# The last 128 dims of the first x chunk: a DMA transposition replaced by a row load and four matmuls

## The chip, the cores and the metric

The kernel runs on one core of a Trainium2 chip. The metric is the device time of one execution in microseconds. The profile is one execution on the chip; its times count from the start of the profiled span. TensorE (PE) multiplies, ScalarE (ACT), VectorE (DVE) and GpSimd (POOL) work on tiles, and SyncE (SP) issues nearly all DMAs; ScalarE issues a few at the start on a queue of its own.

## What is computed

One input x of 2048 tokens by 448 dims goes two ways, and a gate mixes the results:

```
x = A_x
g = sigmoid((x * gate_w).sum(-1, keepdims=True))
a = A_ref(x, wq, wk, wv, wo, beta)   # 16 heads of 28 dims, 4 segments of 512 tokens
b = B_ref(x, w1, b1, w2, b2)         # layernorm, then an MLP over the token axis, F = 1792
return g * a + (1 - g) * b
```

In A each segment has causal softmax attention inside it (`p = softmax(q k^T * scale + mask)`, `a_dot = p v`), and a linear memory of the segments before it (`a_mem = phi(q) M / phi(q) z`). Both are mixed by a sigmoid of beta per head and go through wo. B normalizes x over its dims, multiplies over tokens with w1 (`u = h^T w1 + b1`), applies gelu and multiplies with w2. All inputs are bf16.

## The kernel before

**Two forms of x.** The projections q, k and v contract over dims, so they need x with dims on the partitions: `xT`, four chunks `c` of up to 128 dims by 2048 tokens. The chunks begin at dims 0, 128, 256 and 320 (`C0`, line 21), so the last two overlap. The layernorm and the MLP need x with tokens on the partitions: `xh`, 16 tiles of 128 tokens. `xT` is made by DMA transpositions straight from memory (`transpose_x`, line 533). For each block `tc` of 512 tokens there are two: `dtx{tc}_0` for chunks 0 to 2, and `dtx{tc}_1` for chunk 3. Each is a resource of its own, `R_xT[tc][0]` and `R_xT[tc][1]`. `xh` is loaded by `load_x` (line 519), four tiles at a time: `ldx0`, `ldx4`, `ldx8`, `ldx12`.

**The order of the work.** Every operation has a name and is put in a list with what it reads and writes (`Sched.op`). A table `ORDER` (lines 304 to 376) gives the order of the names on each engine, written out in full. `@4` behind a name is the PSUM bank that it takes out of banks 4 to 7; `u0-7*6` is six matmuls from number 7 on. `Sched.plan` follows the table, and `finalize` puts semaphore waits where an operation reads what another engine or a DMA made. Each engine works through its row in order. On TensorE, `mm` (line 279) issues all matmuls of projections and MLP, so they all bear line 282.

**The start, on TensorE.** `warm` is nine 512-wide matmuls on constants into bank 3 (line 651). `gtr` (lines 839 and 840) transposes the gate's weights, which `gw` on VectorE copies out. `warm2` is one more warm-up. Then the v projection of token tiles 0 to 3: `pra0` to `pra3` take chunk 0 and the first piece of wv, `prb0` to `prb3` chunk 1 and the second piece. `lot2`, `lot0`, `prt0` to `prt3` take chunks 2 and 3 with the rest of wv. A group is made by `pair` (line 680). Of chunks 2 and 3, which overlap, each pair of tiles uses one as a whole and 64 rows of the other; the two halves run side by side in the array (`lo`, 64 rows, which the profile shows as 64\*128). After v come the k and q projections of block 0 (`prk0_*`, `prx0_3`, `prq0_*`), which wait for weights that VectorE copies into a padded form (`padk`, `padx`, `padq`, line 662), and then block 1. Scores of the first segment (`sc0_*`, line 973), block 2's k projections (`prk2_*`) and the MLP (`u*`) are interleaved behind them. `prk2_1`, the first of block 2, waits for both transpositions of that block. ScalarE turns scores into exponentials (`exp0_*`, line 982), out of PSUM banks 0 to 3, which the next scores use again. The scores are shown as 28\*128.

**The start, on the DMA queues.** SyncE's row begins `dtx0_0 dtx0_1 ldwk0 ldwk1 ldwq0 ldwqb dtx1_0 dtx1_1 ldx0 ldx4 ldx8 ldbeta ldw1_0_0 dtx2_0 ldx12 dtx2_1`. ScalarE issues the four pieces of wv, a piece of wk, and small loads (lines 525, 529, 546, 555, 557).

Of the kernel before, what the change touches and what calls it, by code (L numbers as in the profile page):

```python
# [12 lines left out]
D = 448  # L13
# [292 lines left out]
warm gtr@4 warm2 pra0@7 pra1@4 pra2@5 pra3@6 prb3 prb2 prb0 prb1 lot2 lot0 prt1 prt3 prt2 prt0 pra0_1 pra0_2 pra0_0  # L306
btr@7 lok0_0 lok0_2 prk0_0 prx0_3 prk0_2 prk0_1 prt7@4 prx1_3@5 prk1_2@6 lot6@7 lok1_2 loq0_0 loq0_2 prq0_2 prq0_0
prt6 prq1_2@4 prq0_2h prq1_1@5 prq1_2h@6 loq1_0@7 loq1_2 prq0_1 prq1_0 prk1_1@4 sc0_0 lok1_0@5 lot4@67 prk1_0 prt5
prt4 sc0_1 prk2_1@4 prx2_3@5 prk2_2@6 lok2_2 lok2_0@7 sc0_2 prk2_0 u1-0@6*5 u0-0@4 u1-5 u0-1*2 u2-0@5*3 sc0_3 u0-3
u2-3*2 u0-4*2 u3-0@7*2 u0-6 u2-5*2 u3-2 u1-6 sc0_4 u1-7 u0-7*6 u3-3 u0-13 u2-7 u3-4 u0-14*2 u1-8 sc1_0 u1-9*6 u2-8*2  # L310
u1-15 u2-10*4 u3-5*2 u4-0@4 u3-7*2 sc1_1 u5-0@6*2 u2-14 u5-2*2 u2-15 u3-9*6 u5-4 u3-15 u4-1*5 u5-5*2 pv1@5 u4-6*2
sc1_2 u4-8 u5-7*5 u4-9*4 u5-12 pv0@7 u5-13 sc1_3 u4-13*3 u6-0@5*3 u7-0@7 u6-3 u5-14 u6-4*2 u5-15 u6-6 sc1_4 u6-7
u7-1 u6-8*4 u7-2*2 u6-12 u7-4*3 u6-13*3 sc2_0 u7-7*7 pv2@4 u7-14*2 sc2_1 mst0@6 u8-0@4*2 prq2_1@5 prq2_0@7 loq2_0
sc2_2 u8-2*4 prq2_2@5 u8-6*4 prq2_2h@6 loq2_2 mem1 u8-10*2 u9-0@5 u8-12 u9-1*8 u8-13*2 u11-0@6 sc2_3 u9-9*3 pv3@7
u9-12 u8-15 u9-13*2 u11-1 u9-15 u11-2*4 sc2_4 u10-0@7*3 u11-6*6 u13-0@4 u10-3 pv4@5 sc3_0 u10-4*12 u11-12 u13-1
sc3_1 u13-2*3 u11-13*2 u13-5*2 pv5@5 u11-15 prt9@7 u13-7*4 sc3_2 lot8@5 u13-11*2 u12-0@6*5 prt8 u13-13*3 u12-5 sc3_3
lot10@57 u12-6*3 prt11 u12-9*7 prt10 sc3_4 mst1@7 prk3_1@4 pv6@6 prk3_0@7 lok3_0 sc4_0 prq3_1@5 prq3_0@7 wo0@6
# [7 lines left out]
y10-10*2 y11-9*3 y10-12 y11-12*2 lw14@45 y10-13 wo14 wo15 wo12@7 y12-0@6*2 lw12@5 wo13 y13-0@4*4 y15-0@7 y13-4*2  # L325
y14-0@5*2 y13-6*4 y12-2 y14-2*2 y13-10 y14-4 y12-3*2 y13-11 y12-5*3 y14-5 y15-1 y12-8*3 y14-6*3 y13-12*2 y12-11*3
y14-9*5 y15-2*12 y15-0#1@4 y15-1#1 y15-2#1 y15-3#1 y15-4#1 y15-5#1 y15-6#1 y15-7#1 y15-8#1 y15-9#1 y15-10#1 y15-11#1
# [25 lines left out]
ag7 fin5 mq3_3 phq3_2 oa10 ta11 rec11 msta2 phq3_3 oa11 mstc2 om11 tm12 tm13 tm14 tm15 ot11 ot10 cpv15 cpv14 eps13
fin4 ta12 eps15 gcol3 b2g2 eps12 omg3 rec12 oa12 fin6 ag8 om12 ta13 ot12 rec13 fin7 om13 oa13 o13 ot13 eps14 fin8
ag10 ta14 rec14 om14 oa14 ta15 rec15 om15 oa15 b2g3 fin9 ot14 ot15 fin11 fin10 fin13 fin12 fin14 fin15 fin15#1""",
# [9 lines left out]
dtx0_0 dtx0_1 ldwk0@0 ldwk1 ldwq0@1 ldwqb dtx1_0 dtx1_1 ldx0 ldx4 ldx8 ldbeta ldw1_0_0 dtx2_0 ldx12 dtx2_1 ldw1_0_1  # L365
# [13 lines left out]
def build_kernel(nc, X, WQ, WK, WV, WO, BETA, W1, B1, W2, B2, GW, OUT):  # L379
# [139 lines left out]
    def load_x(eng, t0, n):  # L519
        op(eng, lambda e: e.dma_start(xh[:, t0 : t0 + n, :], xv[:, t0 : t0 + n, :]),  # L520
           writes=R_x[t0 : t0 + n], name=f"ldx{t0}", dma=True, cost=500, nbytes=n * 128 * 896, prio=-3)
# [310 lines left out]
    def do_gw():  # L832
# [5 lines left out]
        def fn(e):  # L838
# [456 lines left out]
```

## Time and profile before

| what | us |
|---|---|
| median of three runs | 170.68 |
| lowest and highest of the three | 170.39, 171.07 |
| the profiled execution | 170.68 |
| its span, from the first to the last instruction | 168.9 |
| TensorE busy in the span | 164.7 |
| VectorE busy | 136.7 |
| ScalarE busy | 130.6 |
| GpSimd busy | 64.3 |

A matmul's duration runs from its issue to its modelled end; the next one can start before that, so the distance between starts tells the rate. PEld are the weight loads, which run beside matmuls. An engine name with q behind it (SPq, ACTq) is the engine's issuing side: the duration is the time that the issue took, not the transfer. `t` stands for any tile of the kernel. "t<-t L282" and the like name the line and not the operation, so operations are told by their time, their shape and their place in the row.

### The profile page before, as it was taken

To read this page: it belongs to the slowest core of one execution; us is meant where nothing else is said; L and a number is where in the kernel's file an instruction comes from. 1 tells how busy PE (TensorE), PEld (TensorE's weight loads), DVE (VectorE), ACT (ScalarE), POOL (GpSimd) and SP (SyncE) were. 2 spreads that over 40 slices of the span, in tenths; PEclk is the share of its full clock that TensorE was granted. 3 is DMA by queue.
4 is the path that set the end of the run, shared out by engine and by line. 5 is a ranking of instruction groups with operands and counts; after the bars stand their busy time and mean duration, and the time that the engine had idled before them with its cause. 6 is when DMAs were issued, how large, how long until landed. Compare 5 with 4: busy or idle time off the path is not lost.

```text
span 168.9 us, 4944 instructions
## 1 busy us (share of the span) xinstructions
PE 164.7 (98%) x2022; PEld 78.5 (47%) x2026; DVE 136.7 (81%) x321; ACT 130.6 (77%) x164; POOL 64.3 (38%) x100
## 2 busy tenths in 40 slices
PE   8999999999999999999999999999999999999994
PEld 2334444444554644544453454444454444564553
DVE  0088999877989989999999999999999978695042
ACT  0359999999999997999999998988985788604100
POOL 5000245260442524142177356445837355540000
PEclk9999999999999999999999999999999999999999
DMA  6998999888699945994337302328853129831202
GB/s 144 249 258 289 248 153 246 160 228 226 138 167 254 222 101 146 163 213 124 109 98 169 82 4 65 94 82 111 244 148 110 46 70 280 229 103 60 84 27 82
DMA packets 53974, 25.44 MB, mean 151 GB/s; under 512 B 18416, under 2 KB 53712, under 8 KB 53952
## 3 DMA queue, kind: packets, MB, share of 16 engines
q1 hardware_dynamic: 53160, 24.54, 61.2%
q10 hardware_dynamic: 792, 0.58, 1.7%
q8 instruction: 16, 0.26, 0.7%
q14 instruction: 6, 0.05, 0.1%
HBM read 18.82 MB, written 2.36 MB: 125 GB/s over the span
## 4 chain that ended last, share of the span: by engine, by line
PE 94%; DMA 3%; ACTq 1%; issue 1%; POOL 0%; DVE 0%; POOLq 0%
PE t L282 79%; PE t L973 8%; PE t L1003 5%; DMA t<-in_A_wv_dram 3%; PE t L856 1%; PE t L1076 1%; ACTq L525 1%; ACTq L546 0%; DVE t L1165 0%; POOL t L544 0%; POOL t L620 0%; POOL t L587 0%; POOL t L619 0%; POOL t L615 0%; POOLq L1280 0%
## 5 line engine op out<-in xcount | busy, mean ns | idle before, releaser
L282 PE MATMUL t<-t 128*32 128x448 bf16 (+9 forms) x1257 | 140.4, 352 | 1.0 <-issue 0.6
L282 PEld LDWEIGHTS t<-t 128*32 128x32 bf16 (+2 forms) x1261 | 63.7, 97 | 63.8 <-issue 15.3
L982 ACT ACTIVATE t<-t 128x2048 bf16<-128x2048 f32 x40 | 75.2, 1879 | 6.8 <-PE t L973 6.2
L985 POOL TENSOR_SCALAR_AFFINE_SELECT t<-t 128x512 bf16<-128x512 bf16 x64 | 43.3, 688 | 43.0 <-ACT t L982 40.0
L1040 POOL TENSOR_TENSOR t<-t 128x448 bf16<-128x448 f32 (+2 forms) x13 | 13.3, 1026 | 19.0 <-DVE t L1033 14.4
L1165 DVE SCALAR_TENSOR_TENSOR t<-t 128x448 bf16<-128x448 f32 (+2 forms) x17 | 10.7, 642 | 10.6 <-PE t L282 10.5
L973 PE MATMUL t<-t 28*128 28x512 bf16 (+3 forms) x256 | 15.8, 301 | 0.0
L1017 DVE STREAM_TRANSPOSE t<-t 128x512 f32<-128x512 f32 x16 | 11.3, 706 | 2.9 <-PE t L1003 2.7
L925 POOL TENSOR_TENSOR t<-t 128x4 f32<-128x4 f32 x4 | 4.2, 1054 | 23.4 <-DVE t L923 21.4
L1119 ACT ACTIVATE t<-t 128x448 bf16<-128x448 f32 x10 | 7.1, 732 | 7.6 <-PE t L282 7.6
L1003 PE MATMUL t<-t 128*32 128x512 bf16 (+3 forms) x256 | 11.5, 300 | 0.0
L1059 DVE STREAM_TRANSPOSE t<-t 128x512 bf16<-128x512 bf16 x16 | 10.9, 690 | 0.0
L973 PEld LDWEIGHTS t<-t 28*128 28x128 bf16 x256 | 4.4, 92 | 14.0 <-ACT t L982 7.7
L818 ACT ACTIVATE t<-t 128x448 bf16<-128x448 f32 x13 | 6.8, 546 | 4.2 <-PE t L282 4.2
L916 DVE BATCH_NORM_STATS2 t<-t 128x6 f32<-128x448 bf16 x16 | 9.3, 610 | 0.7 <-DMA t<-in_A_x_dram 0.7
L1145 DVE SCALAR_TENSOR_TENSOR t<-t 128x448 f32<-128x448 f32 x14 | 9.0, 649 | 0.7 <-ACT t L1140 0.6
L1003 PEld LDWEIGHTS t<-t 128*32 128x32 bf16 x256 | 6.7, 96 | 5.3 <-issue 0.7
L1137 ACT ACTIVATE t<-t 128x448 f32<-128x448 f32 x14 | 8.8, 638 | 0.1
L779 ACT ACTIVATE t<-t 128x512 bf16<-128x512 bf16 x12 | 7.6, 635 | 1.4 <-DVE t L736 1.4
L808 DVE SCALAR_TENSOR_TENSOR t<-t 128x512 bf16<-128x512 bf16 x12 | 8.5, 712 | 0.1
L1143 DVE TENSOR_SCALAR t<-t 128x448 f32<-128x448 f32 x10 | 6.5, 676 | 2.4 <-ACT t L1137 2.3
L1033 DVE SCALAR_TENSOR_TENSOR t<-t 128x448 f32<-128x448 f32 x12 | 8.4, 699 | 0.0
(76 smaller groups left out, 132.1 us busy)
## 6 DMA issues: line engine op xcount, KB each, us to landing
t<-in_B_w_dram SPq DMA_DIRECT2D x52, 256.0 KB, 3.9
t<-in_A_x_dram SPq DMA_DIRECT2D x4, 448.0 KB, 5.4
out_dram<-t SPq DMA_DIRECT2D x15, 112.0 KB, 2.0
t<-in_B_w_dram SPq DMA_DIRECT2D x8, 128.0 KB, 2.5
t<-in_A_wv_dram ACTq DMA_DIRECT2D x4, 112.0 KB, 4.1
t<-in_A_wq_dram SPq DMA_DIRECT2D x1, 336.0 KB, 4.8
spare_heads<-t SPq DMA_DIRECT2D x8, 32.0 KB
spare_heads<-t SPq DMA_DIRECT2D x16, 16.0 KB
```

Source lines behind the costliest of these rows:

```text
L282: last = e.matmul(out[q], w[:, q], x, skip_group_check=True, **kw)
L916: op("DVE", lambda e: e.bn_stats(st6[:, t, :], xh[:, t, :]), reads=[R_x[t]], writes=[R_st6[t]], name=f"bns{t}", cost=512, prio=P_PROJ - 10 ...
L973: last = e.matmul(bank(hl)[:, c0 : c0 + w], kT[r, hg, s * 512 + j * 128 : s * 512 + j * 128 + 128], qT[r, hg, s * 512 + 128 * j : s * 512 ...
L982: op("ACT", lambda e: e.activation(pslot(g), ps[:, 0:4, :], ACT.Exp, scale=SCALE), reads=R_bank[0:4], writes=[g.res], take=g, name=f"exp{p ...
L985: op("POOL", lambda e, c0=c0: e.affine_select(pslot(g)[:, :, c0 : c0 + 128], pslot(g)[:, :, c0 : c0 + 128], pattern=[[0, 4], [1, 128]], co ...
L1003: last = e.matmul(bank(cb)[32 * ((hl + hg) % 4) : 32 * ((hl + hg) % 4) + 32, 128 * j : 512], vaug[:, 4 * s + j, 32 * h : 32 * h + 32], psl ...
L1017: dv(lambda e: e.transpose(tt[:, ia, :], bank(cb)[:, 0:512]), [bres(cb)], [R_tt[ia]], "ta", 630, use=(cb,))
L1040: return e.tensor_tensor(dst, part(n3[0]), part(n3[1]), op=ALU.add)
L1059: dv(lambda e: e.transpose(oT[:, hg, s * 512 : s * 512 + 512], o), [R_ob[hg]] + ([R_obx] if hg else []), qres(hg, s), "ot", 635)
L1137: op("ACT", lambda e: e.activation(gg[:, q, :], bank(b)[:, 0:D], ACT.Square, bias=b1s[:, ft : ft + 1], scale=math.sqrt(GC)), **buse(b), re ...
L1145: op("DVE", lambda e: e.scalar_tensor_tensor(gg[:, q, :], gg[:, q, :], 1.0, vh[:, q, :], op0=ALU.add, op1=ALU.mult), reads=[R_gg[q], R_vh[ ...
L1165: op("DVE", lambda e: e.scalar_tensor_tensor(outst[:, p, c0:c1], bank(b)[:, 0 : c1 - c0], omg[:, T : T + 1], ag(T)[:, c0:c1], op0=ALU.mult ...
```

## The change

For block 0, chunk 3 of `xT` no longer comes from a DMA transposition. `dtx0_1` is dropped. In its place the last 128 dims (320 to 447) of the first four tiles of `xh` are loaded as rows by a DMA of its own, `ldxl`, which is the first on SyncE's queue. Later `ldx0` loads only the first 320 dims of those tiles. When `ldxl` has landed, TensorE multiplies each of the four 128 by 128 tiles with an identity matrix (`xtl`, into bank 2), and VectorE copies the four results into `xT` (`cpxl`). `warm2` has two matmuls instead of one. The layernorm's `bns0` to `bns3` read `ldxl`'s columns too.

```
+    R_xl = R("xl")
+
-    def load_x(eng, t0, n):
-        op(eng, lambda e: e.dma_start(xh[:, t0 : t0 + n, :], xv[:, t0 : t0 + n, :]),
-           writes=R_x[t0 : t0 + n], name=f"ldx{t0}", dma=True, cost=500, nbytes=n * 128 * 896, prio=-3)
+    def load_x(eng, t0, n, c0=0, c1=D, writes=None, name=None):
+        op(eng, lambda e: e.dma_start(xh[:, t0 : t0 + n, c0:c1], xv[:, t0 : t0 + n, c0:c1]),
+           writes=writes or R_x[t0 : t0 + n], name=name or f"ldx{t0}", dma=True, cost=500, nbytes=n * 256 * (c1 - c0), prio=-3)
...
-        for k, (c, n) in enumerate(((0, 3), (3, 1))):
+        for k, (c, n) in enumerate(((0, 3), (3, 1))[: 2 if tc else 1]):
...
+    load_x("SP", 0, 4, C0[3], D, [R_xl], "ldxl")
     transpose_x(0)
...
-    load_x("SP", 0, 4)
+    load_x("SP", 0, 4, 0, C0[3])
...
-    warm_up(1, "warm2", P_PROJ + 0.01, 3500.0)
+    warm_up(2, "warm2", P_PROJ + 0.01, 3500.0)
...
+    def last_dims():
+        def fn(e):
+            for t in range(4):
+                last = e.matmul(bank(2)[:, t * 128 : t * 128 + 128], xh[:, t, C0[3] : D], ident[:, :], start=True, stop=True,
+                                skip_group_check=True)
+            return last
+
+        op("PE", fn, reads=[R_xl, R_ident], writes=[R_bank[2]], name="xtl", mode="f", cost=4 * pe_cost(128), prio=P_PROJ - 1)
+        op("DVE", lambda e: e.tensor_copy(xT[:, 3, 0:512], bank(2)[:, 0:512]), reads=[R_bank[2]], writes=[R_xT[0][1]],
+           name="cpxl", cost=dve_cost(512), prio=P_BASE)
```

The table's rows are rewritten with few moves. One line of TensorE's and one of SyncE's, before and now:

```
-warm gtr@4 warm2 pra0@7 pra1@4 pra2@5 pra3@6 prb3 prb2 prb0 prb1 lot2 lot0 prt1 prt3 prt2 prt0 pra0_1 pra0_2 pra0_0
+warm gtr@4 warm2 xtl pra0@4 pra1@5 pra2@6 pra3@7 prb3 prb2 prb0 prb1 lot2 lot0 prt1 prt3 prt2 prt0 pra0_1 pra0_2
-dtx0_0 dtx0_1 ldwk0@0 ldwk1 ldwq0@1 ldwqb dtx1_0 dtx1_1 ldx0 ldx4 ldx8 ldbeta ldw1_0_0 dtx2_0 ldx12 dtx2_1 ldw1_0_1
+ldxl dtx0_0 ldwk0@0 ldwk1 ldwq0@1 ldwqb dtx1_0 dtx1_1 ldx0 ldx4 ldx8 ldbeta ldw1_0_0 dtx2_0 ldx12 dtx2_1 ldw1_0_1
```

Elsewhere the table moves single matmuls inside the MLP (`u2-8`, `u6-6` one place ahead of a group of scores or of another `u`; `y15-0` some ten places later) and a few neighbours on VectorE and SyncE.

TensorE's row at the start of the program, before (L651 is the warm-up, L839 and L840 the gate, the 449-wide matmuls the v projection of block 0, the 512-wide ones the k projection, L887 the biases):

```order
L651 MATMUL t<-const-bfloat16-1.0 128x512 x9
L839 MATMUL t<-t 128x3
L840 MATMUL t<-t 128x1
L651 MATMUL t<-const-bfloat16-1.0 128x512
L282 MATMUL t<-t 128x449 x16
L282 MATMUL t<-t 128x512 x6
L887 MATMUL t<-t 128x30
```

The same place now, in the changed file's line numbers (L655 is the warm-up, L843 and L844 the gate, L854 the new `xtl`):

```order
L655 MATMUL t<-const-bfloat16-1.0 128x512 x9
L843 MATMUL t<-t 128x3
L844 MATMUL t<-t 128x1
L655 MATMUL t<-const-bfloat16-1.0 128x512 x2
L854 MATMUL t<-t 128x128 x4
L282 MATMUL t<-t 128x449 x16
L282 MATMUL t<-t 128x512 x6
L902 MATMUL t<-t 128x30
```

One warm-up and four narrow matmuls stand between the gate and the first matmul of the v projection; what follows is in the order that it had.

SyncE's row from its start, before (L535 are the transpositions of x, L525 and L529 the weights wk and wq, L520 the loads of `xh`):

```order
L535 DMA_TRANSPOSE t<-in_A_x_dram 128x3x512
L535 DMA_TRANSPOSE t<-in_A_x_dram 128x1x512
L525 DMA t<-in_A_wk_dram 128x2x448
L525 DMA t<-in_A_wk_dram 128x448
L525 DMA t<-in_A_wq_dram 128x3x448
L529 DMA t<-in_A_wq_dram 128x448
L535 DMA_TRANSPOSE t<-in_A_x_dram 128x3x512
L535 DMA_TRANSPOSE t<-in_A_x_dram 128x1x512
L520 DMA t<-in_A_x_dram 128x4x448 x3
```

The same place now (L523 are the row loads of x, L538 the transpositions, L528 and L532 the weights):

```order
L523 DMA t<-in_A_x_dram 128x4x128
L538 DMA_TRANSPOSE t<-in_A_x_dram 128x3x512
L528 DMA t<-in_A_wk_dram 128x2x448
L528 DMA t<-in_A_wk_dram 128x448
L528 DMA t<-in_A_wq_dram 128x3x448
L532 DMA t<-in_A_wq_dram 128x448
L538 DMA_TRANSPOSE t<-in_A_x_dram 128x3x512
L538 DMA_TRANSPOSE t<-in_A_x_dram 128x1x512
L523 DMA t<-in_A_x_dram 128x4x320
L523 DMA t<-in_A_x_dram 128x4x448 x2
```

The row load takes the first place, `dtx0_0` goes from first to second, `dtx0_1` is gone, and everything from the load of wk on keeps its place; `ldx0` is narrower.

More of the change, by code (lines that the diff above doesn't have):

```diff
@@ L311 @@
[L311 to L315, printed above, removed]
@@ L915, in ln_stats @@
     def ln_stats(t):
[L916 removed]
+        op("DVE", lambda e: e.bn_stats(st6[:, t, :], xh[:, t, :]), reads=[R_x[t]] + ([R_xl] if t < 4 else []), writes=[R_st6[t]], name=f"bns{t}",
            cost=512, prio=P_PROJ - 10, rel=7500.0)
```

62 lines of the change are left out of this document (34 added, 28 removed).

## The prediction

> **What bounds the kernel now.** The page comes first: how busy is each engine, and of what is the chain that ended last made.
>
> ```profile
> PE 164.7 (98%) x2022; PEld 78.5 (47%) x2026; DVE 136.7 (81%) x321; ACT 130.6 (77%) x164; POOL 64.3 (38%) x100
> PE 94%; DMA 3%; ACTq 1%; issue 1%; POOL 0%; DVE 0%; POOLq 0%
> ```
>
> TensorE is busy 98% of 168.9 us and 94% of the chain is its matmuls. The DMA share, 3%, lies in one piece at the beginning, which the chain in order of time shows:
>
> ```profile
> 2.96 4.43 DMA t<-in_A_wv_dram
> ...
> 8.95 1.47 PE t L282 x6
> ```
>
> The last piece of wv lands at 2.96 + 4.43 = 7.39 us. Behind that the program is a stream of matmuls, and only two things can move its end: when that stream gets going, and the few places where it still stands. The timeline of TensorE shows the beginning (start, duration, both in us; what it waited for in brackets):
>
> ```profile
> 0.82 4.00 PE L651 MATMUL t<-const-bfloat16-1.0 128*128 128x512 bf16 x9 [0.82 <-PEq L1280]
> 4.62 0.21 PE L839 MATMUL t<-t 128*128 128x3 bf16 x1
> 4.69 0.16 PE L840 MATMUL t<-t 128*128 128x1 bf16 x1
> 4.72 0.59 PE L651 MATMUL t<-const-bfloat16-1.0 128*128 128x512 bf16 x1
> 5.21 2.02 PE L282 MATMUL t<-t 128*128 128x449 bf16 x8
> 7.52 2.03 PE L282 MATMUL t<-t 64*128 64x449 bf16 x10 [0.29 <-DMA t<-in_A_wv_dram]
> ```
>
> Nine warm-up matmuls start from 0.82 to 4.62, so 0.42 us apart. Then come the gate's two, one more warm-up, and at 5.21 the first eight matmuls on x (`pra`, `prb`: dims 0 to 255). The ninth, `lot2`, needs the last dims of x and the last piece of wv. The waits between 7 and 7.6 us name both:
>
> ```profile
> PEld t L282 <- DMA t<-in_A_x_dram: 0.7, 1, 0.7
> PE t L282 <- DMA t<-in_A_wv_dram: 0.3, 1, 0.3
> ```
>
> The durations of those eight differ (the first, then the last six; min/median/max in ns):
>
> ```profile
> L282 PE MATMUL t<-t x1: 534/534/534, 5.2 to 5.2; 128*128 128x449 bf16 x1
> L282 PE MATMUL t<-t x6: 352/352/363, 5.9 to 6.9; 128*128 128x449 bf16 x6
> ```
>
> Until about 5.9 us the array is at half rate; afterwards a 449-wide matmul starts every (6.9 - 5.9)/5, about 0.19 us. The eighth started at 6.9 and was through at about 7.07, so the stall ahead of `lot2` is 0.45 us, although the wait rows give 0.3 beside modelled ends.
>
> **The change part by part.** *SyncE's queue.* The two transpositions of the first 512 tokens, their issues apart, and later transpositions on the same queue:
>
> ```profile
> 0.79 1.39 SPq L535 DMA_TRANSPOSE t<-in_A_x_dram  x1
> 2.24 1.25 SPq L535 DMA_TRANSPOSE t<-in_A_x_dram  x1
> ...
> 12.52 4.91 SPq L535 DMA_TRANSPOSE t<-in_A_x_dram  x1
> ...
> 18.10 1.18 SPq L535 DMA_TRANSPOSE t<-in_A_x_dram  x1
> L520 SPq DMA_DIRECT2D t<-in_A_x_dram x4: 507/544/582, 9.7 to 17.5; - x4
> ```
>
> The second, 1.25 us, goes; `ldxl` is of the form of the x loads, 0.54 us, and goes first. Hence `dtx0_0` is issued at about 1.4 instead of 0.79, and everything behind it 1.25 - 0.54, about 0.7 us sooner. The same DMAs' times to landing (the issues at 0.79, 2.24 and 18.10, each alone in its window):
>
> ```profile
> t<-in_A_x_dram SPq DMA_TRANSPOSE x1, 3.7
> t<-in_A_x_dram SPq DMA_TRANSPOSE x1, 5.0
> t<-in_A_x_dram SPq DMA_TRANSPOSE x1, 6.0
> ```
>
> `dtx0_0` landed at 4.5, and would at 5.1 with the same 3.7; `dtx0_1` at 7.2, 0.2 ahead of the last piece of wv (7.39). Removing the transposition alone therefore buys no more than that wait's remainder: wv's piece would be late next, at 7.39, on the other queue. It has one competitor fewer there, so I take it to land no later.
>
> *The row load itself* moves 512 rows of 256 B. In windows of 256 B pieces and of 896 B pieces the DMA engines moved:
>
> ```profile
> DMA packets 857, 0.22 MB, mean 272 GB/s; under 512 B 857, under 2 KB 857, under 8 KB 857
> DMA packets 422, 0.36 MB, mean 364 GB/s; under 512 B 16, under 2 KB 422, under 8 KB 422
> ```
>
> The transposition's pieces were of 256 B as well, so 131 KB cost about 131/272 = 0.48 us of all engines in either form; now they move while the queue is still empty, and `ldx0` loses those columns (131 KB, 0.36 us at 364). The DMA stream is thus some 0.4 us ahead later on. The Trainium skill, "DMA: Bandwidth & Descriptors", section Specifications, speaks against such a load: it wants at least 512 B per piece for the full rate. The trace agrees in direction (272 against 364 GB/s). By that rule the load is inefficient; it would not change the sum, in which the removed pieces count the same.
>
> *TensorE.* Added are one warm-up matmul and the four of `xtl`. The warm-up costs 0.42 (half rate, as above). `xtl` isn't in the trace. Its bounds: four times the 0.07 between L839 and L840, 0.28, where almost no columns are streamed; and four times a weight load that isn't hidden:
>
> ```profile
> L651 PEld LDWEIGHTS t<-const-bfloat16-1.0 x10: 102/147/147, 0.8 to 4.7; 128*128 128x128 bf16 x10
> ```
>
> 4 x 0.147 = 0.59. A quarter of a 512-wide warm-up is 0.105, so four are 0.42; I take 0.45, nearest to that. The first `pra` moves from 5.21 to 5.21 + 0.42 + 0.45 = 6.08. Its data (5.1) and wv's first piece are there by then. Now all eight run at the full rate: 8 x 0.19 = 1.52, to 7.60. `lot2` adds the change from whole rows to half rows of the array: the rows of the scores at 30 us, below, give (30.42 - 30.09) less the 0.21 that a 512-wide matmul takes at the full rate (half of 0.42), about 0.1. So `lot2` is at 7.70, against 7.52: **+0.18**. The stall and the cold start hid most of the added 0.87.
>
> *The copy.* `cpxl` stands behind `gw` on VectorE. Its form is in the trace:
>
> ```profile
> L736 DVE CAST t<-t x4: 652/675/693, 11.3 to 91.0; 128x512 bf16<-128x512 f32 x4
> 8.43 0.47 DVE L662 COPY t<-t 128x784 bf16<-128x784 bf16 x2 [3.36 <-DMA t<-in_A_wk_dram]
> ```
>
> VectorE is idle 3.36 us ahead of 8.43, so nothing is queued behind it that is ready. It starts behind `xtl`, at about 6.1, and ends at 6.8, 0.9 before `lot2`. If `xtl` were late by more than that, `lot2` would be late by the rest.
>
> *The next stands.* The second row is also the next wait: the copies of wk that end at 8.9, for which the matmul of 8.95 waits.
>
> ```profile
> 8.59 0.75 PE L282 MATMUL t<-t 128*128 128x449 bf16 x2
> ```
>
> The last v matmul of this group starts at 8.59 and frees the array at 8.78, so 0.17 is lost. wk is issued 0.7 sooner, and its copies end before 8.7 if it lands only 0.2 sooner: this wait goes, and with it the +0.18. At 8.95 the stream stands where it did, **0.0**.
>
> The third is at 24 us, where the chunk of tokens 1024 to 1535 begins (TensorE's timeline, then the wait row of that stretch):
>
> ```profile
> 23.51 0.40 PE L973 MATMUL t<-t 28*128 28x384 bf16 x8
> 24.16 2.64 PE L282 MATMUL t<-t 128*128 128x512 bf16 x13 [0.26 <-issue]
> 26.73 0.40 PE L973 MATMUL t<-t 28*128 28x256 bf16 x8
> 30.09 0.40 PE L973 MATMUL t<-t 28*128 28x512 bf16 x4
> 30.42 0.93 PE L282 MATMUL t<-t 128*128 128x448 bf16 x4
> PEld t L282 <- issue: 0.5, 1, 0.5
> ```
>
> The releaser reads "issue", but `prk2_1` needs the last dims of x of that chunk: `dtx2_1`, issued at 18.10, landing 6.0 later, at 24.1, and the matmul came at 24.16. Without it the scores' eight (four at a time: 0.16 for 384 columns and 0.06 for 128, as shares of 0.21, and 0.1 for the change) would let it start at 23.84. With the DMA stream 0.4 ahead it lands at about 23.7, and the 0.32 go. What is late next is ScalarE, whose exponentials free the scores' banks:
>
> ```profile
> 24.56 1.87 ACT L982 ACTIVATE t<-t 128x2048 bf16<-128x2048 f32 x1
> 26.63 0.60 ACT L734 ACTIVATE t<-t 128x512 bf16<-128x512 f32 x1 [0.20 <-PE t L282]
> 28.08 1.90 ACT L982 ACTIVATE t<-t 128x2048 bf16<-128x2048 f32 x1
> ```
>
> The scores at 26.73 need the exponential that ends at 26.43, and there ScalarE waits 0.20 for TensorE, which goes too. The next one then ends at 29.8 instead of 29.98, and its scores start some 0.06 behind: 29.84 instead of 30.09. So of 0.32, **0.25** arrive. I see no further stand on a DMA after it, so this reaches the end.
>
> The sum: +0.18 - 0.18 - 0.25 = -0.25, a span of 168.65 for 168.9. The profiled execution took 170.68 (1.78 outside the span), which is also the median of the runs, 170.39 to 171.07: 170.43, so 170.4. The other moves in the tables (`u2-8`, `u6-6`, `y15-0`, a few on SyncE) change places inside runs of like matmuls; I price them at nothing, since no row there waits for a DMA and the number of changes of array form stays.
>
> **The rivals.** *The last transposition isn't sooner.* SyncE stood 4.91 us in the issue of `dtx2_0`: the queue there goes at the DMA engines' pace, and the 0.7 us at the front may be lost in it. Then 24.16 stays and the sum is 0: 170.7 (with half the gain, 170.55).
>
> *Slower: `dtx0_0` is the new stall.* It goes from first to second place, and now meets wv's pieces. It decides from 6.08: whatever it lands later delays the first `pra` and everything behind it. At 5.0 us to landing, that of `dtx0_1`, it lands at 6.4: +0.3, which eats the gain, 170.7. At 6.0 it lands at 7.4: 168.65 + 1.3 + 1.78 = 171.7. For it: the two transpositions behind it took that long. Against: they had its own pieces ahead of them; it has only the row load.
>
> *Faster: the added matmuls cost half.* If the array reached the full rate at about 4.8, the warm-up and `xtl` would cost 0.21 + 0.22, `pra` would start at 5.6 and `lot2` at 7.3, once wv is there: 0.2 sooner at 8.95. ScalarE waits for the scores only 0.14 at 21.2 (its exponential starts at 21.22 behind an end at 21.07), so no more than that is added: about 170.25. Against it: the rows show the half rate until 5.9.
>
> ```profile
> 20.70 0.37 ACT L796 ACTIVATE t<-t 128x256 bf16<-128x256 f32 x1
> 21.22 1.88 ACT L982 ACTIVATE t<-t 128x2048 bf16<-128x2048 f32 x1
> ```
>
> The Trainium skill, "TensorE: Matmul & The Clock Gate", section Part 1, has the full rate come about 4 us into sustained matmuls, give or take 0.5: from 0.82 that is 4.8. This trace differs, 5.1 us into them, so it is a rival and not the forecast.
>
> **How the numbers follow.** Half a per cent, 0.85 us, is about what a measurement of this kernel can tell from no change. Forecast, 170.3 to 170.6: 0.60. No sooner transposition, 170.7: 0.17. `dtx0_0` late, 170.7 to 171.7: 0.14, of which 0.05 beyond 171.53. Added matmuls cheap, 170.25: 0.09. Runs of one kernel scatter by 0.35 to either side; with that the cases reach from 169.8 to 171.2, leaving out most of the late `dtx0_0`. Faster by over 0.5% (under 169.83) needs the cheap matmuls and the scatter: 0.06. Slower by over 0.5%: 0.06. Within: 0.88.
>
> **What would show it.** Right: first `pra` at 6.0 to 6.2 without an idle bracket, all its durations near 0.35; `lot2` at 7.6 to 7.8; no wait on wk at 8.95; `prk2_1` at about 23.85; scores at 29.8 to 29.9. Wrong: a DMA bracket before the first `pra` (the late transposition), a DMA bracket at `lot2` (wv's piece), or `prk2_1` still at 24.1. A span that moves by over 0.5 us either way would come from a place that I haven't named.

## The result and the profile after

| | before | after |
|---|---|---|
| median of six runs, us | 170.8 | 174.19 |
| lowest and highest, us | 170.12, 171.07 | 172.13, 176.33 |
| profiled execution, us | 170.68 | 174.36 |
| its span, us | 168.9 | 172.5 |

The ratio is 1.0151, with a 95% interval of 1.0107 to 1.0194: 1.5% slower, where no change had been forecast. The ratios, here and below, leave out executions over 1.5% above the fastest of their kernel: here the two of 176.3 (with them the medians, 174.19 and 170.8, are 2.0% apart), one each in experiments 1, 4 and 9, three in experiment 11, and one of the kernel before (236.75) beside experiments 13 to 15. The span of the profiled execution grew by 3.6 us.

The page of the changed kernel: the engines' busy time, and the chain by engine.

```profile
PE 166.0 (96%) x2026; PEld 78.9 (46%) x2031; DVE 137.5 (80%) x322; ACT 130.4 (76%) x164; POOL 63.7 (37%) x100
PE 93%; DMA 4%; issue 0%; SPq 0%; DVE 0%
```

TensorE is busy 1.3 us longer, for 3.6 lost: most of it must be standing. The DMA share of the chain has risen from 3% to 4%, and the chain in order of time (start, duration) says which transfer it is now:

```profile
1.30 7.26 DMA t<-in_A_x_dram
8.61 5.68 PE t L282 x22
```

Before, the chain's DMA was the last piece of wv, and it joined TensorE at 7.52, at `lot2`, after the first eight v matmuls had been done. Now it begins with `dtx0_0`, issued at 1.30, and TensorE's first work on x hangs on it. TensorE's timeline at the beginning:

```profile
4.87 0.59 PE L655 MATMUL t<-const-bfloat16-1.0 128*128 128x512 bf16 x2
5.30 0.38 PE L854 MATMUL t<-t 128*128 128x128 bf16 x4
8.61 5.68 PE L282 MATMUL t<-t 128*128 128x449 bf16 x22 [2.92 <-DMA t<-in_A_x_dram]
14.27 1.79 PE L282 MATMUL t<-t 64*128 64x512 bf16 x9
```

The two warm-ups and `xtl` are through at 5.68. Then the array stands for 2.92 us. The 22 matmuls behind it took 5.68 us, and a table by stretches says why (length; busy time of PE, PEld, DVE, ACT, POOL; granted clock; DMA share; GB/s):

```profile
4.55:7.95 3.40, 1.08 (x9) 0.47 (x8) 0.87 (x2) 1.28 (x1) 0.00 (x0) 1.00 1.21 174
7.96:11.36 3.40, 2.75 (x8) 1.04 (x8) 0.47 (x2) 0.00 (x0) 0.00 (x0) 0.50 1.15 319
11.37:14.70 3.33, 3.33 (x21) 1.21 (x19) 1.66 (x9) 1.83 (x7) 0.00 (x0) 1.00 0.98 249
```

In the first stretch TensorE worked 1.08 us of 3.40; in the next one the clock was granted at 0.50, and eight matmuls filled 2.75 us; then it was back. So the late transfer is paid twice. The forecast had the first `pra` at 6.08 and, from there, no loss at 8.95. Now it came 8.61 - 6.08 = 2.53 later, and of the 2.76 us of work from 8.61 to 11.37 at half rate, half was lost: 1.38. The sum, 3.91, is what the timeline shows at the chunk's scores, 24.68 for 20.77 before. The timeline there and further on:

```profile
24.68 0.39 PE L988 MATMUL t<-t 28*128 28x512 bf16 x4
...
27.75 2.65 PE L282 MATMUL t<-t 128*128 128x512 bf16 x13
30.39 0.40 PE L988 MATMUL t<-t 28*128 28x256 bf16 x8
```

The matmuls of 27.75 carry no idle bracket, where before those of 24.16 had 0.26. At 30.39 for 26.73 the loss is 3.66, so 0.25 has been made up, and 3.66 is the end's 3.6 but for 0.06. The size is the forecast's, the reason is not: the transfer that this chunk waited for before, `dtx2_1`, was issued at 19.04 instead of 18.10 and landed 5.6 later, at 24.6 instead of 24.1.

```profile
19.04 1.18 SPq L538 DMA_TRANSPOSE t<-in_A_x_dram  x1
t<-in_A_x_dram SPq DMA_TRANSPOSE x1, 5.6
```

TensorE came to it 3.6 us late, and so no longer waited. What is to be explained lies ahead of 11.4: the late start at 8.61 and the half rate behind it.

SyncE's first issues (start, time in the issue) and, below, the times to landing of `dtx0_0` and of wv's last piece, issued at 2.76:

```profile
0.79 0.45 SPq L523 DMA_DIRECT2D t<-in_A_x_dram  x1
1.30 1.85 SPq L538 DMA_TRANSPOSE t<-in_A_x_dram  x1
3.21 1.07 SPq L528 DMA_DIRECT2D t<-in_A_wk_dram  x2
```

```profile
t<-in_A_x_dram SPq DMA_TRANSPOSE x1, 7.3
t<-in_A_wv_dram ACTq DMA_DIRECT2D x1, 112.0 KB, 6.0
```

`dtx0_0` was issued 0.51 later than before, about as forecast, and took 7.3 us to land instead of 3.7. wv's last piece landed at 8.8 instead of 7.39: not one transfer but both are late. What the DMA engines did shows it best. First a window of before, from 2.5 to 4 us, while `dtx0_0` was landing:

```profile
DMA packets 1514, 0.41 MB, mean 274 GB/s; under 512 B 1463, under 2 KB 1514, under 8 KB 1514
q1 hardware_dynamic: 1449, 0.36, 109.9%
q10 hardware_dynamic: 65, 0.05, 12.1%
```

q1 is SyncE's queue, q10 ScalarE's (the columns: packets, MB, their time as a share of 16 engines). The changed kernel from 4 to 6 us, while `dtx0_0` was under way there:

```profile
DMA packets 841, 0.27 MB, mean 133 GB/s; under 512 B 759, under 2 KB 841, under 8 KB 841
q1 hardware_dynamic: 750, 0.19, 91.4%
q10 hardware_dynamic: 91, 0.07, 30.4%
```

Small pieces in both, but half the rate. A packet of q1 took 1.099 x 16 x 1.5 us / 1449 = 0.018 us before, and 0.914 x 16 x 2 us / 750 = 0.039 us after. The engines are occupied, and each packet takes twice as long.

### The profile page after: what moved, and what is told of

It is laid out like the page before. It is cut to its first block, busy times and chain, and to the rows that moved or that the text cites. A ratio compares the mean times of both kernels' runs of the same rounds, so it can differ in the third digit from the quotient of the medians.

```text
span 172.5 us, 4954 instructions
## 1 busy us (share of the span) xinstructions
PE 166.0 (96%) x2026; PEld 78.9 (46%) x2031; DVE 137.5 (80%) x322; ACT 130.4 (76%) x164; POOL 63.7 (37%) x100
## 4 chain that ended last, share of the span: by engine, by line
PE 93%; DMA 4%; issue 0%; SPq 0%; DVE 0%
PE t L282 79%; PE t L988 8%; PE t L1018 5%; DMA t<-in_A_x_dram 4%; PE t L871 1%; PE t L1091 1%; SPq L523 0%; DVE t L1180 0%; PE t L902 0%
## 5 line engine op out<-in xcount | busy, mean ns | idle before, releaser
L282 PE MATMUL t<-t 128*32 128x448 bf16 (+8 forms) x1256 | 141.2, 353 | 3.3 <-DMA t<-in_A_x_dram 2.9
L1000 POOL TENSOR_SCALAR_AFFINE_SELECT t<-t 128x512 bf16<-128x512 bf16 x64 | 42.8, 680 | 44.5 <-ACT t L997 41.5
L1160 DVE SCALAR_TENSOR_TENSOR t<-t 128x448 f32<-128x448 f32 x14 | 9.5, 683 | 0.8 <-ACT t L1155 0.7
L1048 DVE SCALAR_TENSOR_TENSOR t<-t 128x448 f32<-128x448 f32 x12 | 8.4, 698 | 0.0
L1165 DVE SCALAR_TENSOR_TENSOR t<-t 128x448 bf16<-128x448 f32 x14 | 8.4, 615 | 0.0
```

Of the source, the lines that this page charges most:

```text
L282: last = e.matmul(out[q], w[:, q], x, skip_group_check=True, **kw)
L1000: op("POOL", lambda e, c0=c0: e.affine_select(pslot(g)[:, :, c0 : c0 + 128], pslot(g)[:, :, c0 : c0 + 128], pattern=[[0, 4], [1, 128]], co ...
L1160: op("DVE", lambda e: e.scalar_tensor_tensor(gg[:, q, :], gg[:, q, :], 1.0, vh[:, q, :], op0=ALU.add, op1=ALU.mult), reads=[R_gg[q], R_vh[ ...
```

## The experiments

Three theories were set against each other. **A:** a transposition that is in flight together with rows of ScalarE's queue is slow; half a microsecond of delay moved `dtx0_0` into wv's pieces. **B:** the row load's own bytes ahead of it are the cost. **C:** a transposition is slow beside any rows, whichever queue they come from. "k" below is the first 64-row, 512-wide matmul of the k projection, at 10.37 before and 14.27 after: a good mark, behind all early stands.

**1. The transposition first again, the row load second (from after).**

```
-ldxl dtx0_0 ldwk0@0 ldwk1 ...
+dtx0_0 ldxl ldwk0@0 ldwk1 ...
```

> Only change against the changed kernel: the transposition of chunks 0 to 2 is first on SyncE's queue again and the row load second. Theory A (overlap): the transposition was late because its pieces met the pieces of wv from ScalarE's queue, which begin to flow at about 3.5 us; issued at 0.8 again it lands at 4.4 to 4.7, nothing stalls ahead of the v projection, the array keeps its rate, and the time is 170.2 to 170.9, as in the prediction. Theory B (bytes): the row load's 512 short pieces themselves make the DMA engines slow; they then delay what comes behind, the transposition lands at over 5.5 or the row load lands so late that its four matmuls stall the array, and the time stays over 171.5.

Measured: 171.83 us, ratio 1.0096 (1.0058 to 1.0133). TensorE's timeline, and the DMA engines from 6 to 8 us:

```profile
6.88 0.40 PE L854 MATMUL t<-t 128*128 128x128 bf16 x4 [1.60 <-DMA t<-in_A_x_dram]
```

```profile
DMA packets 935, 0.72 MB, mean 358 GB/s; under 512 B 153, under 2 KB 935, under 8 KB 935
q1 hardware_dynamic: 683, 0.55, 81.3%
q10 hardware_dynamic: 252, 0.17, 25.9%
```

`dtx0_0` landed 3.9 us behind its issue (3.7 before the change), as A says. The time was missed all the same: as the second DMA, the row load took 4.6 us, landed at 6.84 and held up `xtl`, 1.60 us. Rows of both queues (782 of the 935 pieces of 512 B or more) move at 358 GB/s together, so two queues at once are not what is slow. The late row load and a time over 171.5 are what B had named, so this run alone doesn't decide between the two.

**2. Only the delay, without a row load (from before).**

```
-dtx0_0 dtx0_1 ldwk0@0 ldwk1 ldwq0@1 ldwqb dtx1_0 dtx1_1 ldx0 ldx4 ldx8 ldbeta ...
+ldbeta dtx0_0 dtx0_1 ldwk0@0 ldwk1 ldwq0@1 ldwqb dtx1_0 dtx1_1 ldx0 ldx4 ldx8 ...
```

`ldbeta`, 4 KB, takes the first place, and `dtx0_0` is issued at 1.24.

> The kernel before, with the tiny load of beta (4 KB, about 0.5 us of issue) moved from the tenth place to the first on SyncE's queue, so that the first transposition starts 0.55 us later and nothing else is added. Theory A (overlap): the delay alone puts the transposition into wv's pieces; it lands at 6.5 or later, the v projection starts at that time, and the kernel takes 172 to 176, with a lower clock where the stall is long. Theory B (bytes of the row load): without a row load the transposition lands at 5.1, the first matmul on x waits for nothing or 0.1 us, and the time is 170.5 to 171.2.

Measured: 172.99 us, 1.0131 (1.0091 to 1.0171). The landing of `dtx0_0`, and TensorE's timeline:

```profile
t<-in_A_x_dram SPq DMA_TRANSPOSE x1, 5.8
```

```profile
7.07 5.97 PE L282 MATMUL t<-t 128*128 128x449 bf16 x22 [2.23 <-DMA t<-in_A_x_dram]
```

So the loss doesn't need a row load: 0.45 us of delay makes the kernel before stand 2.23 us at the same place and lose 1.3%, where the change loses 1.5%. Whether a row load adds to it is left open by this run. Its stretch from 7.29 to 10.69 was again at 0.50, which costs 1.70 of the 2.66 that k is late.

**3. No overlap with wv: its later pieces wait until `dtx0_0` has landed (from after).**

```
+               reads=[R_xT[0][0]] if name == "wv" and k else [],
```

> The changed kernel, with the second, third and fourth piece of wv on ScalarE's queue issued only when the transposition of chunks 0 to 2 has landed (a wait on ScalarE's queue), so that no row load of the other queue runs beside it. Theory A (overlap): the transposition, still second in its queue, lands at 4.9 to 5.4; the first four v matmuls start at about 5.7 and the array then stalls at wv's second piece until about 7.5; 171 to 172.5 in all. Theory B (bytes, or the second place in the queue as such): it lands at over 6.5 all the same.

Measured: 178.54 us, 1.0452 (1.0422 to 1.0483). The DMAs issued from 5.3 to 7.5, and TensorE:

```profile
t<-in_A_wv_dram ACTq DMA_DIRECT2D x3, 112.0 KB, 7.1
...
t<-in_A_x_dram SPq DMA_TRANSPOSE x1, 8.9
```

```profile
5.75 0.93 PE L282 MATMUL t<-t 128*128 128x449 bf16 x4 [0.48 <-DMA t<-in_A_x_dram]
12.91 4.16 PE L282 MATMUL t<-t 128*128 128x449 bf16 x12 [6.22 <-DMA t<-in_A_wv_dram]
```

`dtx0_0` landed at 5.7, a little behind A's range and 4.4 behind its issue, so with wv's pieces out of the way the row load ahead of it costs 0.7 and not 3.6. The time was missed badly, and as A would have it: wv's pieces now met the next transposition, `dtx1_0`, and both were late, 7.1 and 8.9 us to landing (`dtx1_0` took 5.5 before). The effect isn't tied to the first transposition.

**4. Sixteen warm-up matmuls instead of two, to keep the clock up (from after).**

```
-    warm_up(2, "warm2", P_PROJ + 0.01, 3500.0)
+    warm_up(16, "warm2", P_PROJ + 0.01, 3500.0)
```

> The changed kernel with 16 matmuls in the second warm-up in place of 2, which fill the array until about 8.5 us and read nothing that is waited for. The transposition is as late as before. If the half rate behind the stall is a cost of its own (eight matmuls at 0.374 us for 0.19, 1.5 us), the v projection starts at 8.5 to 8.7 as before, its matmuls are 0.19 apart, and the time is 172.0 to 172.8 with less scatter than 172.1 to 176.3. If the half rate were not due to the stall, time and scatter stay as they were.

Measured: 173.32 to 174.1 us in three runs, 1.0183 (1.0158 to 1.0209); the profiled execution took 241.98 us, and its trace is not read here. The forecast, 172.0 to 172.8, failed. The number of matmuls was too large (16 x 0.21 us from 5.2 reach past 8.5), so it is repeated with nine.

**5. One queue: wv's later pieces behind `dtx0_0` on SyncE's (from after).**

```
-ldwv0 ldgw ldwv1 ldwv2 ldwvb ldwkb ldb1 ldb2 ...
+ldwv0 ldgw ldb1 ldb2 ...
-ldxl dtx0_0 ldwk0@0 ldwk1 ...
+ldxl dtx0_0 ldwv1 ldwv2 ldwvb ldwk0@0 ldwkb ldwk1 ...
```

> The changed kernel, with the second to fourth piece of wv and the last piece of wk moved from ScalarE's queue to SyncE's, right behind the transposition of chunks 0 to 2, which is still second behind the row load. Theory A (overlap of the transposition with rows of another queue): with all rows behind it in its own queue it lands at 5.1 to 5.8, the pieces of wv land at 6 to 7.5, the stall ahead of the v projection is under 0.3 us, the array keeps its rate, and the time is 170.2 to 171.2. Theory C (the transposition is slow beside any rows in flight, whatever their queue): it lands at over 6.5 and the time is over 171.5.

Measured: 171.65 us, 1.0054 (1.0039 to 1.007). TensorE:

```profile
5.52 0.63 PE L854 MATMUL t<-t 128*128 128x128 bf16 x4
5.95 4.70 PE L282 MATMUL t<-t 128*128 128x449 bf16 x22
...
11.37 5.46 PE L282 MATMUL t<-t 64*128 64x512 bf16 x30 [0.34 <-DVE t L666]
```

`dtx0_0` took 4.5 us, and the stand ahead of `pra` is gone, though the same rows follow right behind it on its own queue. A's landing came true. C's did not, but C isn't refuted as it was put: from 3.5 to 4.0 all 551 pieces that moved were under 512 B, and rows appear only from 4.6 on, so behind a transposition on the same queue there are hardly any rows in flight beside it. The time, over A's 171.2, was missed: k starts 0.26 late, and a new wait of 0.34 follows, on VectorE's copies of weights that now queue behind wv.

**6. Nine warm-up matmuls (from after).** The edit is that of experiment 4 with 9.

> The changed kernel with 9 matmuls in the second warm-up in place of 2: the array is busy until about 7.0 us and then waits about 1.5 us, a stall as long as one after which the rate was kept in the run with the transposition first. If the half rate behind the long stall costs 1.5 us where it comes and makes the scatter: 172.0 to 172.8, the v matmuls 0.19 apart, no run over 173. If not, it is as the changed kernel, 172.1 to 176.3.

Measured: 173.51 us, 1.0161 (1.0141 to 1.0181), and the four runs lie within 173.01 to 173.74. TensorE:

```profile
9.15 4.35 PE L282 MATMUL t<-t 128*128 128x449 bf16 x22 [1.19 <-DMA t<-in_A_x_dram]
```

The clock stayed at 1.00, the 22 matmuls took 4.35 instead of 5.68, and the scatter went, as forecast. The level was missed: `dtx0_0` came at 9.11 in this execution, and even the gate's small load was late (a wait of 0.73). Keeping the array busy takes the scatter away, not the late transfer.

**7. One queue without the change (from before).** The same four pieces go to SyncE's queue behind `dtx0_0` and `dtx0_1`.

> The kernel before, with the same four pieces moved to SyncE's queue behind the two transpositions. Theory A: the second transposition, which took 5.0 us to land beside wv's pieces, lands at 5.2 to 6.0 instead of 7.2; wv's last piece, now behind it, lands at 6.8 to 7.6, so the v projection's second half starts within 0.4 of where it did and the time is 170.2 to 171.1. Theory C: the second transposition still lands at 6.5 or later.

Measured: 171.94 us, 1.0067 (1.0047 to 1.0087). `dtx0_1` took 3.6 us to land instead of 5.0: A again, in the kernel before. The time, forecast at 171.1 at most, is lost later, to the weights:

```profile
10.60 0.39 PE L282 MATMUL t<-t 64*128 64x512 bf16 x2 [0.80 <-DVE t L662]
11.64 1.57 PE L282 MATMUL t<-t 64*128 64x512 bf16 x7 [0.65 <-DVE t L662]
```

**8. One queue, the transposition first, one warm-up, `xtl` behind the four `pra` (from after).**

```
-warm gtr@4 warm2 xtl pra0@4 pra1@5 pra2@6 pra3@7 prb3 ...
+warm gtr@4 warm2 pra0@4 pra1@5 pra2@6 pra3@7 xtl prb3 ...
-ldxl dtx0_0 ldwk0@0 ldwk1 ...
+dtx0_0 ldxl ldwv1 ldwv2 ldwvb ldwk0@0 ldwkb ldwk1 ...
```

> Of the changed kernel, with all of the early rows on one queue as in the run above, the transposition first, the row load second, one matmul in the second warm-up, and the four matmuls that turn the rows between the first and second group of v matmuls. Theory A: the transposition lands at 4.5, the row load at 5.1 to 5.8, wv's pieces by 6.8; the v projection starts at 5.2 and its second half at 7.3 to 7.6 without a stall over 0.2; with the wait at the third chunk gone, 169.9 to 170.6, the kernel before being 170.55. Theory C: a stall of over 0.5 ahead of the second group or of the second half, and no gain.

Measured: 171.22 us, 1.0032 (1.002 to 1.0043). The front is even with before:

```profile
6.76 3.66 PE L282 MATMUL t<-t 128*128 128x449 bf16 x18
10.41 2.92 PE L282 MATMUL t<-t 64*128 64x512 bf16 x13
```

k starts at 10.41 for 10.37. Until the first scores (21.16 for 20.77) another 0.35 is lost, 0.3 of it in a wait for copied weights as in experiment 5, and that is more than the third chunk gives. The forecast of 170.6 at most is missed.

**9. Row load on ScalarE's queue, wv's last piece on SyncE's, the rest as in 8 (from after).**

```
-ldwv0 ldgw ldwv1 ldwv2 ldwvb ldwkb ldb1 ldb2 ...
+ldwv0 ldgw ldxl ldwv1 ldwv2 ldwkb ldb1 ldb2 ...
-ldxl dtx0_0 ldwk0@0 ldwk1 ...
+dtx0_0 ldwvb ldwk0@0 ldwk1 ...
```

> Transposition first on SyncE's queue, so that it is through before rows of the other queue flow; behind it rows on both queues: the row load on ScalarE's queue ahead of wv's second and third piece, wv's last piece on SyncE's ahead of wk; one matmul in the second warm-up; the four turning matmuls between the two groups of v matmuls. Theory A: the transposition lands at 4.5 to 4.8, the row load at 5.5 to 6.2, all of wv by 7.0; the v projection starts at 5.2, its second half at 7.2 to 7.5, wk is not later than before; 170.0 to 170.5, with the kernel before at 170.6. If rows ahead of wv's second piece begin early enough to meet the transposition, it lands after 5.5 and the time is over 171.

Measured: 171.21 us over twelve runs (170.11 to 173.51), 1.0015 (0.9997 to 1.0033). The median missed the forecast of 170.0 to 170.5. The profiled execution, 170.41 us, has k at 10.35, and its scores are

```profile
20.75 0.39 PE L988 MATMUL t<-t 28*128 28x512 bf16 x4
...
26.47 0.40 PE L988 MATMUL t<-t 28*128 28x256 bf16 x8
```

TensorE is not late here (20.77 and 26.73 before), `dtx2_1` is issued at 16.91 instead of 18.10, and the stand at the third chunk is gone: 0.26, the forecast's gain, by the forecast's way. It is one execution. Its span of 168.6 equals the shortest of the kernel before on that chip (168.6 to 169.9), and the median doesn't show the gain.

**10. Only wv later: two small loads ahead of its pieces on ScalarE's queue (from after).**

```
-ldwv0 ldgw ldwv1 ldwv2 ldwvb ldwkb ldb1 ldb2 cpv2 ...
+ldwv0 ldgw ldb1 ldb2 ldwv1 ldwv2 ldwvb ldwkb cpv2 ...
```

> The changed kernel with the two small bias loads (7.5 KB, 0.8 us of issue) ahead of wv's second to fourth piece on ScalarE's queue in place of behind the last piece of wk: wv's pieces and the transposition stand to each other in time about as in the kernel before, only all of it 0.6 later. Theory A: the overlap shrinks, the transposition lands at 5.5 to 7.0 instead of 8.6, and the time is 170.8 to 172.5. If the time of wv's pieces has no part in it: 8 to 9 and 172.1 to 176.3 as before.

Measured: 170.92 us over ten runs (170.36 to 171.26), 1.001 (0.9998 to 1.0022). `dtx0_0`'s landing, then TensorE:

```profile
t<-in_A_x_dram SPq DMA_TRANSPOSE x1, 5.4
```

```profile
5.68 0.39 PE L854 MATMUL t<-t 128*128 128x128 bf16 x4
6.73 4.34 PE L282 MATMUL t<-t 128*128 128x449 bf16 x22 [0.66 <-DMA t<-in_A_x_dram]
```

SyncE's queue and TensorE's order are those of the changed kernel; wv's pieces are issued 0.83 us later, from 2.69 instead of 1.86, and the loss is gone: the stand falls from 2.92 to 0.66 and the clock stays up. This is the most direct evidence for A. k is 0.69 late (11.06) and the scores of the third chunk 0.45 (27.18 for 26.73), so 0.24 is made up in between.

**11. The changed kernel once more, on the chip of 9, 10 and 12.**

> The changed kernel once more, unchanged, beside the other three on one chip. Its transposition lands at 7.9 to 9.1 and its runs fall into groups about 1.9 us apart by the number of stretches of 3.4 us at half rate (none, one, two): 172.2, 174.2, 176.3, with mean clocks of 1.00, 0.99 and 0.98.

Measured: 175.04 us (172.37 to 176.52), 1.0187 (1.0138 to 1.0236). So the difference to experiment 10 is no matter of chips. The profiled execution, 176.52 us, by stretches:

```profile
7.16:10.56 3.40, 0.24 (x1) 0.13 (x2) 0.18 (x1) 0.00 (x0) 0.00 (x0) 0.50 1.14 245
10.58:13.97 3.39, 3.39 (x12) 1.03 (x10) 0.46 (x2) 0.00 (x0) 0.00 (x0) 0.50 1.14 268
```

`dtx0_0` landed only at 10.27 (7.9 to 9.1 had been forecast), 9.0 us behind its issue, and two stretches in a row were at half rate. The same sum as above holds: `pra` at 10.31 is 4.23 behind 6.08; half of the 3.66 us from there to 13.97 is 1.83; less 0.25 that is 5.8, and the span of 174.7 is 5.8 over before. So the profiled run of 176 is the same loss with a later landing and a longer half rate. In the first six runs the mean clock goes with the time: 1.00 at 172.1 and 172.4, 0.99 at 174.0 and 174.4, 0.98 at 176.3, which would be none, one and two such stretches. Five of the six runs here lie so too. One, 175.43 at 1.00, doesn't fit, so that the stretches alone make the levels is not shown.

**12. The nine warm-ups again, same chip.**

> The kernel with 9 matmuls in the second warm-up once more, beside the changed kernel on the same chip. If the half rate is what sets the groups apart, all its runs have a mean clock of 1.00 and lie with the lowest group of the changed kernel, to 0.5 us; if the longer warm-up also costs time by itself, they lie 1 us or more above that group, as its first runs (173.0 to 173.7) lay above 172.1.

Measured: 173.86 us (172.85 to 174.13), 1.0173 (1.0144 to 1.0201), the clock at 1.00 in every run, `pra` at 9.42 behind a wait of 1.76. The second case came true in three runs of the four: they lie 1.5 to 1.8 above the changed kernel's lowest (172.37), the fourth 0.5. But it isn't the added matmuls that cost it: they and `xtl` are through at 7.66, and TensorE waits. By the sum of experiment 11, 9.42 - 6.08 - 0.25 = 3.09 over 168.9 gives the measured span of 172.0 without any half rate. So in this execution the landing sets the level; why it came later than in the lowest runs of the changed kernel isn't shown.

**13. The shift of experiment 10 without the change (from before).** The diff is the same line.

> The kernel before with one edit: the two small bias loads ahead of wv's second to fourth piece on ScalarE's queue, as in the run that brought the changed kernel back. Theory A (a transposition and rows of the other queue in flight together are slow): the second transposition no longer meets wv's pieces and lands at 5.2 to 6.0 in place of 7.2; wv's last piece lands at 6.5 to 7.8; time 170.2 to 171.0. If the second transposition was slow for its own form (one chunk wide), it lands at about 7 all the same.

Measured: 171.07 us, 1.0018 (1.0002 to 1.0035). `dtx0_1`, issued at 2.2 as before, took 3.7 us instead of 5.0, as A says, so the kernel before has the overlap as well, in its second transposition; there it cost nothing, since wv's last piece landed later still. `dtx0_0` took 4.3 here and 4.2 in experiment 7, though it was first in its queue: so 3.7 to 4.3 is its spread where wv's later pieces come after it. Moved back, wv's last piece lands at 8.05, over the 7.8 that was forecast, and costs what `dtx0_1` saves; the time is over the 171.0 as well:

```profile
8.16 2.72 PE L282 MATMUL t<-t 64*128 64x449 bf16 x14 [1.06 <-DMA t<-in_A_wv_dram]
```

**14. Experiments 1 and 10 together, one warm-up, `xtl` behind `pra` (from after).** The edits are those shown there and in 8.

> The changed kernel with both: transposition first and row load second on SyncE's queue, wv's second to fourth piece behind the bias loads on ScalarE's, one matmul in the second warm-up, and the turning matmuls between the two groups of v matmuls. Theory A: transposition at 4.4 to 4.7, row load at 5.2 to 6.0, wv's last piece by 7.3; the v projection starts at 5.2, its second half at 7.2 to 7.6, no run at a lower clock; 170.0 to 170.6 against 170.7, that is the 0.25 at the third chunk and little else. If the time is 170.7 or more, the gain that the prediction put at the third chunk is given back elsewhere.

Measured: 171.72 us, 1.0053 (1.0033 to 1.0074). The expected 170.0 to 170.6 failed. `dtx0_0` took 3.9 us, as it should, but all the rows behind were late:

```profile
6.97 0.40 PE L854 MATMUL t<-t 128*128 128x128 bf16 x4 [1.28 <-DMA t<-in_A_x_dram]
9.51 2.72 PE L282 MATMUL t<-t 64*128 64x449 bf16 x14 [0.92 <-DMA t<-in_A_wv_dram]
```

That the rows of both queues then want the engines at once is the likely reading, but not tested. Why wv's later pieces need 5.1 us here (the median of three) and 4.0 in experiment 10 isn't settled.

**15. wv sooner, nothing else (from before).**

```
-ldwv0 ldgw ldwv1 ldwv2 ldwvb ldwkb ...
+ldwv0 ldwv1 ldgw ldwv2 ldwvb ldwkb ...
```

> The kernel before with one edit on ScalarE's queue alone: wv's second piece is issued ahead of the gate's small load in place of behind it, 0.8 us sooner. SyncE's queue is untouched and no row load is added. Theory A: its pieces now meet the first transposition, which lands at 5.5 or later in place of 4.5; the time is 171.2 to 174. If what counts is only the place on SyncE's queue, the first transposition lands at 4.4 to 4.8 and the time is 170.4 to 171.

Measured: 171.09 us over ten runs (170.2 to 172.56), 1.0019 (0.9992 to 1.0046). The landing of `dtx0_0`:

```profile
t<-in_A_x_dram SPq DMA_TRANSPOSE x1, 5.0
```

SyncE's queue is untouched and `dtx0_0` is issued at 0.79, yet it took 5.0 us, for 3.7 to 4.3 elsewhere. So the overlap can be made from the other queue as well. The time, forecast at 171.2 or more, can't be told from that of before: the runs scatter by 2.4 us. In the profiled one (172.21) the late landing cost nothing by itself: the gate's load, now behind wv's piece, held TensorE up for 0.68, to 6.08, and its v matmuls up to 9.2 took 534 to 582 ns each, the half rate's duration, while the clock is given as 1.00. So not every half rate shows in the granted clock.

No version was faster than the kernel before by anything that can be told; 9 and 10 equal it.

## Why the prediction was wrong

**The step that failed** is "`dtx0_0` landed at 4.5, and would at 5.1 with the same 3.7". It took 7.3 us and landed at 8.56. The 3.7 was read off a transposition that moved 274 GB/s nearly alone, and was carried to a place 0.51 us later where wv's pieces were in flight. Shown by experiments 2 (the delay alone), 10 (the other queue alone, the loss gone) and 15 (the other queue alone, the landing late).

**Its twin** is the sentence that wv's piece "has one competitor fewer there, so I take it to land no later". It landed at 8.8 instead of 7.39. Counting competitors is not enough: in this mixture both queues slow down.

**The rival that came true** is "`dtx0_0` is the new stall", held at 0.14. Its place, its cause and its deciding point, 6.08, were right. Its price was not. The bounds, 5.0 and 6.0 us to landing, came from transpositions with other transpositions ahead of them; 7.3 and more were seen. And it counted the stand alone: by its own formula a landing at 8.56 gives 168.65 + 2.5 + 1.78 = 172.9 us, and the other 1.4 of the 174.36 are the half rate behind the stand, which no case had. The reason against it ("they had its own pieces ahead of them; it has only the row load") looked at its own queue and not at the other.

**The bytes of the row load** were priced at 0.48 us of the DMA engines, and at nothing for the landing of `dtx0_0` behind them. With wv's later pieces out of the way it took 4.4 to 4.5 us in experiments 3 and 5, up to 0.8 over the 3.7: a term was missing, but a small one.

**SyncE's queue.** `dtx0_0` was issued at 1.30 (forecast about 1.4). What stands behind it came 0.34 sooner (3.21 for 3.55) and not 0.7, since the transposition's issue took 1.85 us instead of 1.39. Then even that was lost: the issue of `dtx1_0` took 4.54 us instead of 2.67, and the next row loads of x were issued at 11.22 instead of 9.70.

**TensorE's additions.** `xtl` was taken as 0.45. In experiment 5, where all of it ran at half rate, it took 5.95 - 5.52 = 0.43, and the two warm-ups 5.52 - 4.71 = 0.81, so 0.40 each for 0.42. In the changed kernel the full rate came sooner (the two warm-ups start 0.43 before `xtl`, so 0.21 each), so the condition of the rival "added matmuls cost half" did hold, and bought nothing, since `pra` had no data.

**The +0.18 at `lot2` and the -0.18 at 8.95** could not be seen in the changed kernel, whose first matmuls came too late for both.

**The third chunk.** 0.25 forecast, 3.91 - 3.66 = 0.25 measured, and about the same in experiment 10 (0.69 - 0.45). In the changed kernel this agreement is luck. "The DMA stream is thus some 0.4 us ahead later on" was wrong there: `dtx2_1` landed at 24.6, 0.5 later than before. The stand went because TensorE was later still, and it goes in the same way without the change: from the first scores to those of the third chunk it is 5.96 us before, 5.72 in experiment 2 and 5.71 in experiment 13. Only experiment 9, where TensorE is on time and `dtx2_1` ahead, shows the gain as it was meant. The reading that ScalarE limits it from there held (its exponential ends at 30.33, the scores start at 30.39).

So the gain was of the right size but did not come as forecast; the price was 3.9 us in place of nothing. The mechanism behind that is shown down to the overlap of the two queues. Two things stay open. Why the DMA engines take twice as long per packet in that mixture isn't visible in the trace. And the length varies: 5.0 and 5.8 us to landing without a row load (experiments 15 and 2), 7.3 to 9.0 with the row load ahead (after, experiments 6, 11 and 12). All of the second group are longer, so the row load may well add to the overlap; whether it does, or how near wv's pieces are issued, or scatter, wasn't told apart.

## What to carry to other kernels

The time that a DMA took to land belongs to its place among the transfers of all queues, and not to the DMA alone: before you move one, draw what the other queue has in flight at the new place, and price the landing from a row in which that same mixture occurs. A long stand of TensorE is to be priced with the clock behind it, here up to 1.7 us for each half-rate stretch: it followed stands of 2.23 us and more, and none of up to 1.76. Where a change puts an early transfer at risk, try the cheap counter-move on the other queue first: here two small loads swapped with wv's pieces took the whole loss away.

## What the runs showed of the hardware

- A transposition of SyncE's queue beside row loads of ScalarE's: 133 GB/s in all, 0.039 us per packet of the transposition (after, 4 to 6 us); nearly alone 274 GB/s and 0.018 us (before, 2.5 to 4); row loads of both queues, 358 GB/s (experiment 1, 6 to 8). The Trainium skill, "DMA: Bandwidth & Descriptors", section Issuing engines are not separate DMA queues, says that DMAs of all issuing engines run on the same 16 DMA engines and interleave. The traces agree that they share; that the sum falls to half in one mixture it doesn't say, and here that decided the time.
- The half rate that the granted clock shows comes in stretches of 3.40 us (7.96 to 11.36 after; 7.29 to 10.69 in experiment 2; two in a row in 11). In the 3.40 us ahead of the first, TensorE had worked 1.08, 1.17 and 1.49 us; in experiment 1 it worked 1.79 us in such a stretch, and the clock stayed:

```profile
4.64:8.04 3.40, 1.79 (x14) 0.88 (x13) 0.89 (x3) 1.28 (x1) 0.00 (x0) 1.00 1.06 329
```

  The Trainium skill, "TensorE: Matmul & The Clock Gate", section Part 1, has windows of about 3.4 us, and the half clock after a window that was idle. The length agrees. But the window need not be wholly idle: a stand of 2.23 us was enough in experiment 2, and one of 1.60 in experiment 1 or 1.76 in experiment 12 was not. The amount of work isn't the whole rule: in experiment 14 TensorE worked only 1.33 us from 5.69 to 9.09, in several pieces, and the clock stayed; where a window begins can't be seen while the clock stays.
- The issue of `dtx0_0` took 1.39 us as the first DMA of its queue, and 1.83 to 2.18 behind the row load (after, experiments 3, 5, 6, 10, 11 and 12).
